# First blocks' last 64 features on VectorE, their fronts in another order, first weight jobs in other sizes, second block's end later

## The chip, the cores and the metric

One core of a Trainium2 chip runs the kernel. The metric is the device time of one execution in microseconds, the median of several runs. Engines: PE (TensorE; PEld is its weight load), DVE (VectorE), ACT (ScalarE), POOL (GpSimd) and SP (SyncE, which here only issues transfers).

## What is computed

Three layers, one after the other, on 2 x 4096 tokens of 192 features in float32:

```python
w = softmax(weight)                       # 8 heads x 7 taps; 24 features share a head
x = causal depthwise convolution of x with w, 7 taps
gate = 1 / (1 + exp(-(x @ w_gate)))       # 192 x 1536
x = (gate * (x @ w_val)) @ w_out          # 1536 x 192
h = x @ w_in                              # 192 x 2048
x = where(h > 0, h, exp(min(h, 0)) - 1) @ w_out2    # 2048 x 192
```

The weights arrive as 64-bit floats.

## The kernel before

**Tiling.** Tokens are cut into 16 blocks of 512. A block's 192 features lie as tiles of 128 rows: n holds features 0 to 127, s the same with its two halves of 64 rows swapped (made by two transfers inside the chip), r the last 64 features, in both halves. A matmul here uses 64 rows of PE, and two of them, on the two halves, run side by side; that is what n, s and r are for. Every value is split in a high part with few bits and the rest (h = cast on ACT, l = value - h on DVE), and a product is taken as three of four partial products. The same holds for the weights: w1 (gate and value), w2 (out), w3 and w4 of the second layer, each as h and l.

**A step.** A step is (kind, block, j): kind 1 is the gated layer, kind 2 the other. `front` (L345) runs 18 matmuls of 64 x 512 into two banks: gate and value of 128 hidden features, or 2 x 128 of kind 2. ACT and DVE make g from them (e by sigmoid, g = e x value; or relu, exp and g), split g into gh and gl, and two steps later (LAG) `back` (L397) multiplies them with w2 or w4 into the banks a0 to a3. Blocks 0 and 1 go together: their steps alternate, and one `back` of 20 matmuls serves both. 24 steps of kind 1 for blocks 0 and 1 (about 3.2 us each), 12 for block 2, 16 of kind 2 for blocks 0 and 1, 8 for block 2; then the next group. `end1` takes a block's sums out of the banks and makes n, s, r of kind 2.

**The convolution.** Later blocks are convolved on DVE, seven instructions over a tile (`conv`, L167), in time for their steps. For blocks 0 and 1, whose values are wanted first, PE does it: `diagonal` (L127) makes diagonal matrices of the tap weights on ACT; `conv_first` (L214) takes the first 128 features of both blocks with 56 matmul records, `conv_third` (L236) the last 64 with 28 such records. `split` (L203) then makes h and l. Two matmuls on zeros stand ahead (L591).

**The weights.** A job (`prep_in` for w1 and w3, `prep_out` for w2 and w4, with `narrow`, L268) turns 64-bit weights into h and l: transfers bring the words into a tile s (two buffers; m in some cases), ACT takes t = |high word|, DVE makes h, then the unit t, then the rest and its low part, ACT casts h. The first six jobs (ROOM, L29) have 384 columns and work within the tile s or m. The later ones have 768 columns and first need a copy m<-s, shifted by two bytes, by a transfer inside the chip; there is one m.

**What sets the order.** The program is recorded by hand: for each half step the pieces due are written out. PREPARED says how many pieces of the jobs are due by which step, CONV at which steps a block's convolution goes on, `times` (L680) when the pieces of an end are. Each engine runs its instructions in this order, and SP sends transfers in it.

Of the kernel before, what the change touches and what calls it, by code (L numbers as in the profile page):

```python
# [28 lines left out]
ROOM = "ssmssm"  # L29
# [8 lines left out]
    (-18, 0), (-15, 10), (-13, 10), (-9, 18), (-5, 18), (-1, 21), (2.5, 31), (6.5, 48.5),  # L38
    (10.5, 65), (14.5, 74.5), (18.5, 89.5), (24, 99), (34.5, 126), (38, 127), (49.5, 160),
# [18 lines left out]
def conv_glu_elu_kernel(  # L58
# [154 lines left out]

    def conv_first():  # L214
# [21 lines left out]
    def conv_third(fold):  # L236


        diagonal(1, fold)
        x = xin_t[0, 1]  # L240
        banks = two_banks()
        for k, w in enumerate(diagonals[1]):
            for acc, rows in zip(banks, HALVES):
# [24 lines left out]
    def narrow(src, out, room):  # L268


        copied = room is None
# [462 lines left out]
```

## Time and profile before

| | us |
|---|---|
| median of 3 runs | 1194.4 (1194.36 to 1194.5) |
| the profiled execution | 1194.23 |
| its span, first to last instruction | 1192.2 |
| PE busy | 1185.0 (99%) |
| DVE busy | 844.0 (71%) |
| ACT busy | 788.7 (66%) |

Matmuls overlap and their ends are modelled, so PE's busy time is read by counts of matmuls and by starts. A timeline row has start, duration, engine, line, operation, what it writes and reads, and in brackets the idle time before it with what ended it. DVE and ACT are busy in part, but not evenly: the first 90 us hold most of the weight jobs.

### The profile page before, as it was taken

Reading aid. Unit: us, or ns where it says so; the run is one execution under the profiler, and the core shown is the slowest. Engines: PE = TensorE matmul, PEld = TensorE weight load, DVE = VectorE, ACT = ScalarE, POOL = GpSimd, SP = SyncE. Lnnn points to the kernel's source line nnn. Section 1 sums busy time; section 2 is a strip of 40 time slices with the busy share of each in tenths; the row PEclk is TensorE's granted clock in tenths of the full one; section 3 lists DMA queues with packets and bytes.
Section 4 is the critical chain, followed back from the end, with each engine's and each line's share of the span. In section 5 each row is a group of like instructions: output and inputs, shape, how many; then the busy total and the mean of one; then the engine's idle time right before and its main releaser. Section 6 shows DMA issues by size and latency. Waiting matters only on the chain.

```text
span 1192.2 us, 25068 instructions
## 1 busy us (share of the span) xinstructions
PE 1185.0 (99%) x10332; PEld 1111.3 (93%) x10332; DVE 844.0 (71%) x1282; ACT 788.7 (66%) x1378; POOL 79.7 (7%) x70
## 2 busy tenths in 40 slices
PE   9999999999999999999999999999999999999998
PEld 4989989888888899999999999999999999999998
DVE  7998689785447877477766677666766667765675
ACT  6556788854448886448854498545884468844686
POOL 0000000001001000011001010010100100001110
PEclk9999999999999999999999999999999999999999
DMA  6656340321001020111112011020110201111100
GB/s 168 215 184 190 103 133 28 90 54 45 5 24 46 19 63 19 28 37 45 28 36 53 12 45 45 19 63 4 43 45 20 63 11 35 45 36 28 28 15 19
DMA packets 31794, 65.26 MB, mean 55 GB/s; under 512 B 4480, under 2 KB 15744, under 8 KB 31680
## 3 DMA queue, kind: packets, MB, share of 16 engines
q1 hardware_dynamic: 31680, 63.66, 19.2%
q8 instruction: 81, 1.33, 0.5%
q14 instruction: 33, 0.27, 0.1%
HBM read 19.74 MB, written 6.29 MB: 22 GB/s over the span
## 4 chain that ended last, share of the span: by engine, by line
PE 95%; DVE 3%; ACT 1%; DMA 1%; issue 1%; DVEq 0%; ACTq 0%
PE ps L343 52%; PE a L343 41%; DMA m<-s 1%; DVE gl L394 1%; PE ps L223 1%; PE ps L244 1%; DVE g L367 0%; DVE g L381 0%; ACT e L378 0%; PE ps L591 0%; ACT e L377 0%; ACT gh L388 0%; DVE w2s L312 0%; DVE t L292 0%; DVE h L298 0%
## 5 line engine op out<-in xcount | busy, mean ns | idle before, releaser
L388 ACT CAST gh<-g 128x512 fp32r<-128x512 f32 x448 | 273.3, 619 | 189.6 <-DVE g L367 147.2
L394 DVE TENSOR_TENSOR gl<-g,gh 128x512 fp32r<-128x512 f32 x448 | 333.1, 757 | 76.6 <-ACT gh L388 64.3
L343 PE MATMUL a<-gh,w4s 64*128 64x512 f32 x1536 | 302.7, 387 | 0.0
L343 PE MATMUL a<-gl,w4s 64*128 64x512 f32 x1024 | 256.7, 387 | 0.2 <-DVE gl L394 0.2
L381 DVE SCALAR_TENSOR_TENSOR g<-e,ps 128x512 f32<-128x512 f32 x256 | 174.1, 686 | 110.2 <-ACT e L378 108.8
L343 PEld LDWEIGHTS a<-gh,w4s 64*128 64x128 f32 x1536 | 225.0, 184 | 8.7 <-ACT two L442 0.3
L343 PE MATMUL a<-gh,w2s 64*128 64x512 f32 x1152 | 230.7, 387 | 0.0
L367 DVE TENSOR_TENSOR g<-e,ps 128x512 f32<-128x512 f32 x192 | 131.6, 685 | 136.1 <-ACT e L365 135.7
L365 ACT ACTIVATE e<-ps 128x512 f32<-128x512 f32 x192 | 114.9, 598 | 160.8 <-PE ps L343 160.0
L343 PE MATMUL a<-gl,w2s 64*128 64x512 f32 x768 | 188.1, 387 | 0.4 <-DVE gl L394 0.4
L343 PEld LDWEIGHTS a<-gl,w4s 64*128 64x128 f32 x1024 | 171.3, 184 | 6.4 <-DVE gl L394 1.2
L343 PEld LDWEIGHTS a<-gh,w2s 64*128 64x128 f32 x1152 | 161.9, 184 | 6.4
L378 ACT ACTIVATE e<-e 128x512 f32<-128x512 f32 x256 | 161.9, 632 | 8.1
L377 ACT ACTIVATE e<-ps 128x512 f32<-128x512 f32 x256 | 150.6, 588 | 15.4 <-PE ps L343 14.7
L343 PE MATMUL ps<-xn,w1h 64*128 64x512 f32 x768 | 152.1, 387 | 0.7 <-DVE g L367 0.7
L343 PE MATMUL ps<-xs,w1h 64*128 64x512 f32 x768 | 151.8, 387 | 0.1
L343 PE MATMUL ps<-xr,w1h 64*128 64x512 f32 x768 | 145.0, 386 | 0.0
L343 PEld LDWEIGHTS a<-gl,w2s 64*128 64x128 f32 x768 | 121.1, 184 | 5.9 <-DVE gl L394 1.7
L343 PEld LDWEIGHTS ps<-xn,w1h 64*128 64x128 f32 x768 | 105.3, 184 | 6.0 <-DVE g L367 1.1
L343 PEld LDWEIGHTS ps<-xs,w1h 64*128 64x128 f32 x768 | 105.1, 184 | 4.7 <-DVE g L367 0.5
L343 PEld LDWEIGHTS ps<-xr,w1h 64*128 64x128 f32 x768 | 102.2, 184 | 4.5 <-DVE xr L209 0.2
L343 PE MATMUL ps<-xn,w1l 64*128 64x512 f32 x384 | 105.2, 386 | 0.0
(107 smaller groups left out, 1728.4 us busy)
## 6 DMA issues: line engine op xcount, KB each, us to landing
xs<-xn SPq DMA_DIRECT2D x61, 256.0 KB, 3.6
m<-s SPq DMA_DIRECT2D x14, 767.8 KB, 4.1
s<-in_w_dram SPq DMA_DIRECT2D x57, 128.0 KB, 3.0
three<-two SPq DMA_DIRECT2D x47, 128.0 KB, 2.2
s<-in_w_dram SPq DMA_DIRECT2D x6, 768.0 KB, 4.6
x<-in_xp_dram SPq DMA_DIRECT2D x16, 259.0 KB, 3.8
out_dram<-one SPq DMA_DIRECT2D x16, 256.0 KB, 2.0
xr<-xr SPq DMA_DIRECT2D x14, 256.0 KB, 3.2
```

The lines of the kernel that those rows point to most:

```text
L223: nc.tensor.matmul(acc[to], w[rows, rows], x[rows, k:k + TB], start=k == 0, stop=k == TAPS - 1)
L244: nc.tensor.matmul(acc, w[rows], x[rows, k:k + TB], start=k == 0, stop=k == TAPS - 1)
L343: return nc.tensor.matmul(ps, w, x, start=first, stop=last)
L365: nc.scalar.activation(s, gate, AF.Sigmoid)
L367: nc.vector.tensor_mul(g, s, val)
L377: nc.scalar.activation(e, h, AF.Relu, scale=-1.0)
L378: nc.scalar.activation(e, e, AF.Exp, scale=-1.0)
L381: nc.vector.scalar_tensor_tensor(g, e, -1.0, h, ALU.add, ALU.max)
L388: nc.scalar.copy(gh, g)
L394: nc.vector.tensor_sub(gl, g, f32(gh))
```

## The change

1. `conv_third` runs on DVE, one multiply and six multiply-adds for the two blocks' 64 features at once, one cast, one subtraction; two transfers make the swapped copy. The 28 matmuls, the second set of diagonals and the matrix `fold` at the start go. Two more matmuls on zeros follow `conv_first`.
2. The x loads of blocks 0 and 1 are issued by ACT, the 64 features' loads by SP directly behind the tap weights.
3. The fronts of the first four steps begin with the parts that no transfer inside the chip makes (n and r for block 0, s and r for block 1), two of them one after the other, and their swapped parts follow. Block 1's first two fronts use the banks a0 to a3.
4. The first jobs: w1 0 and 1 (384 columns), w1 2 and 3 as one job of 768 in m without a copy, w2 0 and 1 (384), then all with a copy; w2 in jobs of 2, 4, 4 and 2.
5. PREPARED and CONV have other numbers. Block 1's end of kind 1 goes on four steps later.

```diff
-ROOM = "ssmssm"
+ROOM = [("s", False), ("s", False), ("m", True), ("s", False)]
...
-    (10.5, 65), (14.5, 74.5), (18.5, 89.5), (24, 99), (34.5, 126), (38, 127), (49.5, 160),
+    (34.5, 127), (38, 129), (49.5, 157),
...
-            nc.sync.dma_start(t, xp[0:P, bi, t0:t0 + TB + PAD])
+            (nc.scalar if b < 2 else nc.sync).dma_start(t, xp[0:P, bi, t0:t0 + TB + PAD])
...
+    def zeros(ps, n):
+        for _ in range(n):
+            nc.tensor.matmul(ps, warm[0][:, 0:P], warm[0], start=True, stop=True)
...
+        zeros(ps_a.tile([P, TB], F32, tag="a3", name="a3"), 2)
         yield
...
-    def conv_third(fold):
...
-        diagonal(1, fold)
+    def conv_third():
...
         x = xin_t[0, 1]
-        banks = two_banks()
-        for k, w in enumerate(diagonals[1]):
-            for acc, rows in zip(banks, HALVES):
-                nc.tensor.matmul(acc, w[rows], x[rows, k:k + TB], start=k == 0, stop=k == TAPS - 1)
-        yield
-        for b in range(2):
-            parts(1, b, "r")
-        yield from split([parts_t[1, b]["r"][0] for b in range(2)], banks)
-        yield
+        acc = xcv.tile([P, TB], F32, tag="xcv1", name="xcv")
+        for k in range(TAPS):
+            w, xk = cwn[:, 1, k:k + 1], x[:, k:k + TB]
+            if k:
+                nc.vector.scalar_tensor_tensor(acc, xk, w, acc, ALU.mult, ALU.add)
+            else:
+                nc.vector.tensor_scalar_mul(acc, xk, w)
+            yield
+        t, other = (xsp.tile([P, 2, TB], F32R, tag="r", name="xr") for _ in HALVES)
...
+        nc.scalar.copy(t[:, 0], acc)
+        yield
+        nc.vector.tensor_sub(t[:, 1], acc, f32(t[:, 0]))
+        for rows, to in zip(HALVES, HALVES[::-1]):
+            nc.sync.dma_start(f32(other)[to], f32(t)[rows])
+        yield
...
-        most, n = 6 * P, 3 * P * (1 + copied)
+        most, n = 6 * P, src.shape[0] * src.shape[2]
...
-        n = slice(n, n + 1 + (room is None))
+        n = slice(n, n + 1 + (room is None or room[1]))
...
-        jobs = [(index[1, 0, j], prep_in, w1d, w1, j) for j in (0, 1, 2, 3, 4, 6, 8, 10)]
-        jobs += [(index[1, 1, j] + LAG, prep_out, w2d, w2s, j) for j in (0, 2, 4, 8)]
+        jobs = [(index[1, 0, j], prep_in, w1d, w1, j) for j in (0, 1, 2, 4, 6, 8, 10)]
+        jobs_2 = [(index[1, 1, j] + LAG, prep_out, w2d, w2s, j) for j in (0, 2, 6, 10)]
...
-        next(jobs[0])
-        next(jobs[1])
         next(load_x(0, 1))
-        next(jobs[2])
+        for n in (0, 1, 2, 2):
+            next(jobs[n])
...
+                if i == 0:
+                    ps = front(w1, 0, parts_t[1, 0], ("nr", "s"), some=range(6))
+                    spare.append(front(w1, 0, parts_t[1, 1], ("sr", "n"), banks(0), range(6)))
+                    return front(w1, 0, parts_t[1, 0], ("nr", "s"), ps, range(6, 9))
+                if i == 1:
+                    return front(w1, 1, parts_t[1, 0], ("nr", "s"))
+                if i == 2:
+                    return front(w1, 0, parts_t[1, 1], ("sr", "n"), spare.pop(), range(6, 9))
+                return front(w1, 1, parts_t[1, 1], ("sr", "n"), banks(2))
...
-                    times = (0.5, 1, 2.5, 3, 3.5) if k == 1 else (0.5, 2.5)
+                    times = (0.5, 2.5) if k == 2 else (4.5, 5, 6.5, 7, 7.5) if b == 1 else (0.5, 1, 2.5, 3, 3.5)
```

**The order on DVE at the start,** from the tap weights (cwn) on; xcv is the convolution's tile, t, h, s and w1l are a weight job's. Before:

```order
L119 TENSOR_TENSOR cwn<-cwe,cwd 128x14
L292 TENSOR_SCALAR t<-t 128x384
L294 TENSOR_SCALAR t<-t 128x384
L298 SCALAR_TENSOR_TENSOR h<-s,t 128x384
L300 TENSOR_SCALAR t<-h 128x384
L306 TENSOR_SCALAR s<-s 128x384
L307 SCALAR_TENSOR_TENSOR s<-s 128x384
L312 SCALAR_TENSOR_TENSOR w1l<-s,t 128x384
L292 TENSOR_SCALAR t<-t 128x384
L294 TENSOR_SCALAR t<-t 128x384
L298 SCALAR_TENSOR_TENSOR h<-s,t 128x384
```

Now, on DVE from the same instruction on:

```order
L121 TENSOR_TENSOR cwn<-cwe,cwd 128x14
L257 TENSOR_SCALAR xcv<-x_104,cwn 128x512
L255 SCALAR_TENSOR_TENSOR xcv<-x_104,cwn,xcv 128x512 x6
L309 TENSOR_SCALAR t<-t 128x384
L311 TENSOR_SCALAR t<-t 128x384
L315 SCALAR_TENSOR_TENSOR h<-s,t 128x384
L264 TENSOR_TENSOR xr<-xcv,xr 128x512
L317 TENSOR_SCALAR t<-h 128x384
L323 TENSOR_SCALAR s<-s 128x384
L324 SCALAR_TENSOR_TENSOR s<-s 128x384
L329 SCALAR_TENSOR_TENSOR w1l<-s,t 128x384
L309 TENSOR_SCALAR t<-t 128x384
```

The seven convolution instructions and the xr split stand ahead of the first job's end and of the xn and xs splits; the two xr splits from banks, further down before, are gone.

**The order on PE around the first fronts** (gh, gl in the first rows are the diagonals; w1h, w1l the weights). Before, the last diagonal matmuls and the first front's start:

```order
L244 MATMUL ps<-x_112,gh 128x512 x8
L244 MATMUL ps<-x_112,gl 128x512 x6
L343 MATMUL ps<-xn,w1h 128x512
L343 MATMUL ps<-xs,w1h 128x512
L343 MATMUL ps<-xn,w1h 128x512
L343 MATMUL ps<-xs,w1h 128x512
L343 MATMUL ps<-xn,w1l 128x512
L343 MATMUL ps<-xs,w1l 128x512
L343 MATMUL ps<-xs,w1h 128x512 x4
L343 MATMUL ps<-xs,w1l 128x512 x2
L343 MATMUL ps<-xr,w1h 128x512 x4
L343 MATMUL ps<-xr,w1l 128x512 x2
```

Now, on PE from the added zeros (warm) behind the first 128 features' matmuls on:

```order
L218 MATMUL a_179<-warm 128x512 x2
L360 MATMUL ps<-xn,w1h 128x512
L360 MATMUL ps<-xs,w1h 128x512
L360 MATMUL ps<-xn,w1h 128x512
L360 MATMUL ps<-xs,w1h 128x512
L360 MATMUL ps<-xr,w1h 128x512 x4
L360 MATMUL ps<-xn,w1l 128x512
L360 MATMUL ps<-xs,w1l 128x512
L360 MATMUL ps<-xr,w1l 128x512 x2
L360 MATMUL a_258<-xs,w1h 128x512
L360 MATMUL a_259<-xn,w1h 128x512
L360 MATMUL a_258<-xs,w1h 128x512
```

The 14 rows' worth of diagonal matmuls on x_112 are gone, r stands ahead of the swapped part, and block 1's first front (a_258, a_259, which are a0 and a1) follows before block 0's is complete; the swapped part (xs in both banks) comes behind it, ten rows below the last one shown.

**The order on DVE at the end of block 2's kind 1 steps** (t, h, m of w3's third job; L381 and L400 make g of kind 2). Before:

```order
L367 TENSOR_TENSOR g<-e,ps 128x512
L292 TENSOR_SCALAR t<-t 128x768
L394 TENSOR_TENSOR gl<-g,gh 128x512
L367 TENSOR_TENSOR g<-e,ps 128x512
L394 TENSOR_TENSOR gl<-g,gh 128x512
L381 SCALAR_TENSOR_TENSOR g<-e,ps 128x512 x2
L394 TENSOR_TENSOR gl<-g,gh 128x512 x2
L381 SCALAR_TENSOR_TENSOR g<-e,ps 128x512 x2
L447 TENSOR_TENSOR one<-a_1511,one 128x512
L447 TENSOR_TENSOR two<-a_1512,two 128x512
L394 TENSOR_TENSOR gl<-g,gh 128x512 x2
L381 SCALAR_TENSOR_TENSOR g<-e,ps 128x512 x2
```

Now, on DVE at the same place, from the same g on:

```order
L386 TENSOR_TENSOR g<-e,ps 128x512
L309 TENSOR_SCALAR t<-t 128x768
L311 TENSOR_SCALAR t<-t 128x768
L315 SCALAR_TENSOR_TENSOR h<-s,t 128x768
L413 TENSOR_TENSOR gl<-g,gh 128x512
L386 TENSOR_TENSOR g<-e,ps 128x512
L317 TENSOR_SCALAR t<-h 128x768
L413 TENSOR_TENSOR gl<-g,gh 128x512
L386 TENSOR_TENSOR g<-e,ps 128x512
L321 TENSOR_SCALAR m<-m 128x768
L413 TENSOR_TENSOR gl<-g,gh 128x512
L400 SCALAR_TENSOR_TENSOR g<-e,ps 128x512 x2
```

The job's steps t, t, h, t, m stand ahead of kind 2's first g; before, its first t alone does.

## Rows read from the trace of the kernel before

**Rows 1.** The page's table of engines: busy us, share, instructions.

```profile
PE 1185.0 (99%) x10332; PEld 1111.3 (93%) x10332; DVE 844.0 (71%) x1282; ACT 788.7 (66%) x1378; POOL 79.7 (7%) x70
```

**Rows 2.** Windows, L343 alone: from:to, us, PE busy (count), granted clock, DMA share, GB/s.

```profile
18.14:32.81 14.67, 13.89 (x110) 1.00 0.64 174
32.81:89.74 56.93, 56.49 (x492) 1.00 0.61 200
89.74:136.24 46.50, 46.50 (x413) 1.00 0.60 182
136.24:216.49 80.25, 79.40 (x671) 1.00 0.22 73
216.49:1187.40 970.91, 970.91 (x8564) 1.00 0.14 35
...
136.24:150.37 14.13, 13.49 (x114) 1.00 0.09 20
```

**Rows 3.** Windows, DVE alone; columns as in rows 2.

```profile
89.20:136.00 46.80, 36.79 (x62) 1.00 0.60 180
146.70:165.00 18.30, 17.52 (x30) 1.00 0.46 134
23.10:89.20 66.10, 64.74 (x114) 1.00 0.60 192
```

**Rows 4.** Timeline of DVE: start, us, what.

```profile
3.62 0.17 DVE L119 TENSOR_TENSOR cwn<-cwe,cwd 128x14 f32<-128x14 f32 x1
7.14 0.36 DVE L292 TENSOR_SCALAR t<-t 128x384 f32<-128x384 f32 x1 [3.35 <-ACT t L285]
7.54 0.36 DVE L294 TENSOR_SCALAR t<-t 128x384 int32<-128x384 int32 x1
7.93 0.56 DVE L298 SCALAR_TENSOR_TENSOR h<-s,t 128x384 int32<-128x384 int32 x1
...
23.08 0.68 DVE L367 TENSOR_TENSOR g<-e,ps 128x512 f32<-128x512 f32 x1
```

**Rows 5.** Timeline of ACT, SP and PE.

```profile
0.74 1.28 ACT L115 ACT_TABLE_LOAD   x1 [0.74 <-PEq L719]
1.19 0.90 SPq L160 DMA_DIRECT2D x<-in_xp_dram  x2
...
18.14 0.79 PE L343 MATMUL ps<-xn,w1h 64*128 64x512 f32 x1
...
32.81 0.75 PE L343 MATMUL ps<-xn,w1h 64*128 64x512 f32 x4
```

**Rows 6.** The chain that ended last: start, us, what.

```profile
12.49 6.21 PE ps L244 x28
```

**Rows 7.** Lines L175 and L179 (convolution of later blocks): count, ns min/median/max.

```profile
L175 DVE SCALAR_TENSOR_TENSOR xcv<-x,cwn,xcv x126: 739/745/787, 46.1 to 1062.4; 128x512 f32<-128x512 f32 x126
...
L179 DVE TENSOR_SCALAR xcv<-x,cwn x19: 478/480/484, 176.2 to 1041.8; 128x512 f32<-128x512 f32 x19
```

**Rows 8.** DMA issues, 0 to 25 us: count, KB each, median us to landing.

```profile
x<-in_xp_dram SPq DMA_DIRECT2D x2, 129.5 KB, 3.0
...
xs<-xs SPq DMA_DIRECT2D x1, 256.0 KB, 4.1
```

**Rows 9.** DVE's groups by shape, 0 to 90 us: busy us, mean ns, idle before.

```profile
L298 DVE SCALAR_TENSOR_TENSOR h<-s,t 128x768 int32<-128x768 int32 x7 | 6.7, 953 | 0.1
L294 DVE TENSOR_SCALAR t<-t 128x768 int32<-128x768 int32 x7 | 3.9, 553 | 0.1
```

**Rows 10.** Waits of PEld, 100 to 216 us: total us, times, longest.

```profile
PEld ps L343 <- DVE g L381: 2.7, 6, 0.8
PEld a L343 <- DVE gl L394: 1.2, 3, 0.7
```

**Rows 11.** Waits over the whole span.

```profile
DVE m L304 <- DMA m<-s: 0.6, 2, 0.3
```

**Rows 12.** Tile m, 0 to 80 us, its transfers.

```profile
DMA to landing us min/median/max: 2.7/4.0/5.2
```

More of the change, by code (lines that the diff above doesn't have):

```diff
@@ L343, in mm, with front @@
         return nc.tensor.matmul(ps, w, x, start=first, stop=last)
-    def front(w, n, x, first):
+    def front(w, n, x, order, ps=None, some=range(9)):
         h, l = (t[:, n] for t in w)
-        ps = [ps_w.tile([P, TB], F32, tag="w", name="ps") for _ in HALVES]
+        ps = ps or [ps_w.tile([P, TB], F32, tag="w", name="ps") for _ in HALVES]
         todo = []
-        for two in ("nsr" if first else ("nr", "s") if w is w1 else ("ns", "r")):
+        for two in order:
             todo += [(part, 0, k) for part in two for k in (0, 1)] + [(part, 1, 0) for part in two]
         for at, (part, low_w, low_x) in enumerate(todo):
+            if at not in some:
+                continue
             wt = l if low_w else h
@@ L551, in conv_glu_elu_kernel @@
         needs, sizes = [x[0] for x in jobs], [6 + (x[1] is prep_out) for x in jobs]
-        takes = [1.0 if n < len(ROOM) else 1.35 for n, size in enumerate(sizes) for _ in range(size)]
+        takes = [1.45 if n == 2 else 1.0 if n < len(ROOM) or x[1:] == jobs_2[3][1:] else 1.35
+                 for n, (x, size) in enumerate(zip(jobs, sizes)) for _ in range(size)]
         jobs = [x[1](*x[2:], dict(enumerate(ROOM)).get(n)) for n, x in enumerate(jobs)]
@@ L562, in weights @@
                 for k, _ in enumerate(f):
-                    if k == (2 if n < 3 else sizes[n] - 1) and n + 1 < len(jobs):
+                    if k == (2 if n == 0 else sizes[n] - 1) and n + 1 < len(jobs):
                         next(jobs[n + 1])
@@ L570, in weights @@
                     next(jobs[n + 1])
-                if one and n + 3 < len(ROOM) + 2:
-                    next(jobs[n + 3])
-                    if n + 3 >= len(ROOM):
-                        next(jobs[n + 3])
+                if one and n != 2:
+                    m = n + 3 - (n == 3)
+                    next(jobs[m])
+                    if m >= len(ROOM):
+                        next(jobs[m])
                 if not one and n + 2 < len(jobs):
@@ L599, in conv_glu_elu_kernel @@
         prepared = weights()
-        for k in range(-40, 2 * len(steps)):
+        for k in range(2 * int(PREPARED[0][0]), 2 * len(steps)):
             for (a, m), (b, n) in zip(PREPARED, PREPARED[1:]):
@@ L618, in conv_glu_elu_kernel @@
         for (b, i), pieces in CONV.items():
-            f = conv(b, i) if b else conv_third(fold) if i else conv_first()
+            f = conv(b, i) if b else conv_third() if i else conv_first()
             if b > 1:
@@ L627, in conv_glu_elu_kernel, with banks @@
         held = {}
+        spare = []
+        def banks(n):
+            return [ps_a.tile([P, TB], F32, tag=f"a{i}", name=f"a{i}") for i in (n, n + 1)]
         for i in range(int(min(extra)) - 1, len(steps) + LAG + 2):
```

44 lines of the change are left out of this document (25 added, 19 removed).

## The prediction

> **What bounds the kernel now.** I read the page's table of engines first: PE is busy for 99% of the span [rows 1], so only time in which PE has no wide matmul to run can be won. Then the windows with the wide matmuls alone (all of `front` and `back`, one line) [rows 2]. From 216 us to the end 8564 of them take 970.91 us, 0.1134 us each, with nothing lost. At that price the other stretches lose: 18.14 to 32.81 us 14.67 - 110 x 0.1134 = 2.2 us; 32.81 to 89.74 us 56.93 - 492 x 0.1134 = 1.1; 89.74 to 136.24 us minus 0.3 (about three matmuls counted reach in from the stretch before); 136.24 to 216.49 us 80.25 - 671 x 0.1134 = 4.2. With those three taken off their counts the second and the fourth lose 1.5 and 4.5 us. Ahead of all this lie 18.14 us without a wide matmul [rows 5]. The change touches these stretches and leaves the rest alone.
>
> What ends the waits is VectorE. From the first g at 23.08 us to 89.2 us it is busy 64.74 of 66.10 us, from 146.7 to 165 us 17.52 of 18.30 [rows 3], and between 100 and 216 us PE waits 2.7 us for its g and 1.2 us for its gl [rows 10]. Earlier it stands still for 3.35 us, until the first weights have come at 7.14 us [rows 4]. So up to 90 us the kernel is a VectorE queue that starts at 7.14 us. PE's own start is the chain of diagonal matmuls, the last 28 of which (the 64 features) take 6.21 us [rows 6].
>
> **The 64 features' matmuls go.** PE loses 6.21 us of work ahead of its first wide matmul. That is no gain by itself: the first front needs xn and xs split, and these now stand behind more work on VectorE.
>
> **The convolution on VectorE.** One multiply of 480 ns and six multiply-adds of 745 ns [rows 7]; each reads what the last one wrote, and such a successor starts some 0.04 us after the end (7.14 + 0.36, then 7.54 [rows 4]): 0.48 + 6 x 0.785 = 5.2 us. When can it begin? The tap weights are ready at 3.62 + 0.17 = 3.8 us [rows 4]. ScalarE now issues two loads ahead of its table load, which took 1.28 us from 0.74 us on; no row shows an issue on ScalarE, but SP takes 0.90 us for these two [rows 5], so exponential and weights come some 0.2 us later: 4.0 us. The 64 features are now SP's second and third transfer, the latter issued at about 1.7 us; such transfers took 3.0 us [rows 8]: 4.7 us. Bounds: 4.0 (landed earlier) and 5.8 (4.1 us, the slowest transfer of rows 8, though that one stays on the chip). I take 4.7, the same kind of transfer. The convolution then ends at 9.9 us. Of its 5.2 us, 2.4 lie in the time in which VectorE stood idle; the other 2.8 push the weights back. One of the two xr splits (0.69 us) goes, and so does about 1 us of waits for ScalarE.
>
> As to those loads, a rule of the Trainium skill speaks against a gain ("DMA: Bandwidth & Descriptors", Issuing engines are not separate DMA queues): whichever engine issues, the same 16 DMA engines carry it, and only issue time is saved. By that rule the x loads would crowd the 64 features', towards the late bound; no row here has two issuers at once. With 5.8 for 4.7 us the sum below would be 1.1 us higher.
>
> **From there to the sixth front.** Ahead of its first g VectorE has two jobs of 384 (each 4 x 0.36 + 3 x 0.56 us [rows 4] = 3.1), six steps of a job of 768 (4 x 0.55 + 2 x 0.95 [rows 9] = 4.1) and three splits of 0.69: 12.4 us. Independent neighbours overlap by some 0.08, dependent ones lose 0.04, which leaves 11.9: the first g at 21.8 us instead of 23.08. PE is no later limit for it: the swapped parts leave when xs is split (9.9 + 6.1 = 16.0 us) and land 4.1 us later [rows 8], at 20.1; with three pairs of matmuls and the sigmoid, g's input is there at 21.7 us. From this g to the fourth VectorE has 17 instructions (seven g, gl of 0.69, one 768 of 0.95, a 384 job, a 0.55), 9.0 us start to start, and one wait: the second e stands behind a cast and a t on ScalarE, 0.9 us. So the fourth g ends at 21.8 + 9.9 = 31.7. It empties the bank a3, which the first `back` needs, because the second block's first fronts now use the a banks; then 7 of that back's 10 pairs remain, 7 x 0.227 = 1.6 us. **The sixth front starts at 33.3 us instead of 32.81 [rows 5]: +0.5.** PE begins earlier and is stopped harder: it waits for the splits, for the swap and for that g, some 1.5 us each time.
>
> **From the sixth front to 89.7 us.** The jobs in other sizes save VectorE time. Between the first g and that of step 20 the new order has, against the old, one 768 multiply-add more (+0.9 us), two 384 less (-1.0), one 384 and two 768 single steps less (-1.3) and two small ones of w2s less (-0.6): 2.0 us less. Before, this stretch filled VectorE; now it falls below PE's pace, and gl is ready 1 to 1.6 us ahead of need. Against it stand the copies m<-s: each may start only when the job before is through with m, it lands in 4.0 us (2.7 to 5.2 [rows 12]), and VectorE asks for it in order. Two jobs (w1 from 4, w1 from 8) have only 3.7 to 4.2 us between; 0.8 to 1 us of standing each, which the lead covers but for some 0.3. Before, all copies together cost 0.6 us [rows 11]. **1.5 lost becomes 0.3: -1.2.** Bounds: -1.5, and 0 (the waits eat the lead).
>
> **From 136 to 216 us.** Five of the six steps of w3's third job now stand ahead of the first fronts of the second kind; before, one did. With what follows from it 2.4 us less of VectorE lie in this stretch. They go to block 2's twelve steps, which get ten 768 instructions more, 6 us; VectorE was busy 36.79 of 46.80 us there [rows 3], so nothing waits. The 4.5 us are not all theirs: up to 150.37 us 14.13 - (114 - 3) x 0.1134 = 1.5 us are lost [rows 2], at the switch of kinds, where e, exp, g and the sums follow one another; these stay. Of the other 3.0 I take **-1.0**, since ScalarE is in those chains too; bounds 0 and -1.9. The second block's end comes four steps later (`times`); that moves three VectorE instructions within the roomy stretch, and its result is used five steps after it is done: nothing.
>
> **Sum.** +0.5 - 1.2 - 1.0 = -1.7 us on the profiled 1194.23 us: 1192.5. The median of the runs, 1194.4, lies 0.2 above: 1192.7, and I say **1192.6 us**, between the two.
>
> **Rivals.**
> 1. *The freed VectorE time is worth all of itself.* Convolution at 4.0 us (-0.7 against the sum), no wait for copies (-0.3), the late stretch at its bound (-0.9): 1190.7. For it: VectorE is full in every stretch that loses. Against: its waits run through ScalarE too.
> 2. *Moved, not removed.* The copies eat the lead (+1.2) and the late stretch is ScalarE's (+1.0): 1194.8, no change. For it: a VectorE step counts only where nothing else is late.
> 3. *Slower: the copy queue.* Place: 30 to 43 us. SP now sends four blocks of w2 and their copy, six fetches for w1 of 0.6 us each, three more, two x loads and the next copy in one row, all behind the swaps. I have that copy land at 42.5 us, 0.8 after VectorE asks. Each us later stops VectorE, and beyond 1.5 us of lead PE; the next copies follow in its wake. Slower than before from about 3 us later on; with 5 us, 3.5 us are lost here and 1 at the job from 8: 1197.1. Against it: all copies before cost 0.6 us [rows 11].
> 4. *The clock.* Waits of 1.5 us between 14 and 31 us could cost PE its rate. In the rows the granted clock is 1.00 (the 2.4 GHz level) in every stretch [rows 2]. At the lower level (1.2 GHz) 40 wide matmuls cost 40 x 0.1134 = 4.5 us more: 1197.1. The Trainium skill ("TensorE: Matmul & The Clock Gate", Why this matters for your kernels) warns that gaps between bursts put PE back to the slow level; by that rule this could happen, and the trace, with shorter gaps, does not show it.
>
> **How the numbers follow.** About 0.2%, 2.4 us, is what a measurement of this kernel can tell from no change: faster means below 1192.0, slower above 1196.8. My forecast (1191.3 to 1193.9) has 0.49, a quarter of it below 1192.0; rival 1 has 0.24, rival 2 0.14, rival 3 0.08, rival 4 0.05. Faster 0.24 + 0.12 = 0.36; slower 0.08 + 0.05 = 0.13; same 0.51. The range for 8 in 10 goes from 1190.2, rival 1 and a little, to 1195.9, the sum with the late bounds (+1.1, +1.2, +1.0); it leaves out rivals 3 and 4 and the tail below.
>
> **What would show it.** Right: VectorE's first multiply at 4.5 to 5 us; the first g near 21.8, the sixth front near 33.3 us; 0 to 0.5 us lost from there to 90 us, 3 to 4 between 136 and 216 us; the first wide matmul well ahead of 18.14 us without gain from it. Wrong: a granted clock below 1; VectorE standing more than 2 us for m; or a sixth front before 32 us, which would mean that the walk has an order or a landing too late.

## The result: 0.9% slower

The changed kernel takes 1204.95 us, median of 6 runs (1203.88 to 1205.4); the kernel before, beside it, 1194.45. The ratio is 1.0088, interval 1.0075 to 1.01: 10.5 us more where 1.8 less were forecast, and outside the range. One of the kernel before's six runs took 2001.79 us; it counts as slow, and the ratio is that of the others. The profiled execution took 1204.93 us. The page's table of engines, to be held against [rows 1]:

```profile
PE 1187.6 (99%) x10308; PEld 1151.1 (96%) x10308; DVE 848.9 (71%) x1280; ACT 785.7 (65%) x1368; POOL 77.6 (6%) x66
```

Busy time tells little: but for PEld no engine has over 5 us more work, and PEld's sum is no measure (1151.1 us here, 1077.2 in e2_late below, with the same weight loads). The windows of the wide matmuls alone (L360 now), cut at the changed kernel's first wide matmul, at its sixth front, at 89.74 and 136.24 us as in [rows 2], and where its last 8564 begin (from:to, us, PE busy (count), PEld busy (count), granted clock, DMA share, GB/s):

```profile
13.80:36.59 22.79, 18.62 (x111) 14.24 (x113) 0.78 0.62 181
36.59:89.74 53.15, 50.48 (x430) 45.94 (x428) 1.00 0.51 168
89.74:136.24 46.50, 45.93 (x400) 41.97 (x398) 1.00 0.65 195
136.24:227.21 90.97, 88.31 (x747) 79.99 (x744) 1.00 0.26 84
227.21:1198.00 970.79, 970.79 (x8564) 964.46 (x8563) 1.00 0.14 35
```

The first wide matmul starts at 13.80 in place of 18.14 us, as forecast without gain: 111 of them then take 22.79 us, at a granted clock of 0.78. The last 8564 take 970.79 us as before. In between, too few matmuls fit into each window.

Since all kernels run the same 10240 wide matmuls, the clearest measure is when the Nth of them starts, in order of starts. The table gives that time minus the kernel before's, in us, from one profile of each kernel. Number 110 (counted from 0) opens the sixth front, 440 starts at 71.7 us before, 542 at 83.3, 962 at 131.0, 1140 at 153.0, 1680 at 216.8. The last columns are the times (median; ratio to the kernel before, 95% interval).

| kernel | 110 | 440 | 542 | 962 | 1140 | 1680 | us | ratio |
|---|---|---|---|---|---|---|---|---|
| changed | +3.8 | +3.3 | +7.1 | +10.2 | +11.5 | +10.7 | 1204.95 | 1.0075 to 1.0100 |
| e1_zeros | +5.0 | +4.0 | +6.8 | +10.7 | +11.6 | +10.7 | 1204.31 | 1.0069 to 1.0100 |
| e2_late | +2.0 | +2.5 | +6.1 | +6.1 | +5.8 | +6.0 | 1201.86 | 1.0049 to 1.0079 |
| e3_times | +2.3 | +2.2 | +5.6 | +10.2 | +10.5 | +9.8 | 1204.18 | 1.0071 to 1.0104 |
| e4_earlier | +3.6 | +3.2 | +3.6 | +6.8 | +8.0 | +7.3 | 1202.56 | 1.0055 to 1.0085 |
| e5_base | +3.9 | +3.6 | +4.0 | +4.0 | +3.6 | +3.8 | 1197.93 | 1.0018 to 1.0040 |
| e6_loads | +2.5 | +3.2 | +3.7 | +3.7 | +3.3 | +3.4 | 1196.98 | 1.0014 to 1.0032 |
| e7_pe_conv | +3.1 | +2.6 | +3.1 | +3.4 | +3.1 | +3.2 | 1197.45 | 1.0022 to 1.0042 |
| e11_pe_conv_t | +3.2 | +2.8 | +3.1 | +3.4 | +3.1 | +3.3 | 1197.52 | 1.0018 to 1.0038 |
| e8_fronts | +3.7 | +4.7 | +5.2 | +5.2 | +4.8 | +5.0 | 1199.20 | 1.0028 to 1.0056 |
| e13_bank | +3.5 | +3.4 | +3.9 | +3.9 | +3.6 | +3.7 | 1197.16 | 1.0015 to 1.0037 |
| e16_zeros2 | +2.3 | +3.0 | +3.5 | +3.5 | +3.1 | +3.3 | 1197.26 | 1.0017 to 1.0038 |
| e14_jobs | +1.7 | +2.5 | +2.9 | +4.2 | +3.9 | +4.0 | 1198.33 | 1.0023 to 1.0049 |
| e15_mended | +0.1 | +0.8 | +1.2 | +1.3 | +1.0 | +1.1 | 1196.33 | 1.0009 to 1.0028 |
| e17_w2_earlier | +1.5 | +2.4 | +2.8 | +2.9 | +2.5 | +2.8 | 1195.27 | 1.0004 to 1.0022 |
| e9_start | +5.3 | +5.3 | +5.3 | +5.2 | +5.2 | +5.2 | 1199.88 | 1.0032 to 1.0062 |
| e10_start_loads | +4.1 | +3.7 | +3.7 | +3.6 | +3.6 | +3.6 | 1198.20 | 1.0021 to 1.0047 |
| e18_start_mended | +3.0 | +2.8 | +2.8 | +2.7 | +2.7 | +2.7 | 1197.64 | 1.0020 to 1.0043 |
| e12_before_late | -0.4 | -0.2 | -0.2 | -0.3 | +0.9 | -0.3 | 1194.68 | 0.9993 to 1.0013 |

The changed kernel loses in three places: 3.8 us ahead of the sixth front, 3.8 between matmuls 440 and 542 (75 to 90 us), 3.1 between 542 and 962 (90 to 141 us); of 1.3 more at the switch of kinds 0.8 come back behind it.

The start, on DVE (timeline; to be held against [rows 4]):

```profile
4.43 0.17 DVE L121 TENSOR_TENSOR cwn<-cwe,cwd 128x14 f32<-128x14 f32 x1
6.25 0.49 DVE L257 TENSOR_SCALAR xcv<-x,cwn 128x512 f32<-128x512 f32 x1 [1.65 <-DMA x<-in_xp_dram]
6.77 4.69 DVE L255 SCALAR_TENSOR_TENSOR xcv<-x,cwn,xcv 128x512 f32<-128x512 f32 x6
11.38 0.35 DVE L309 TENSOR_SCALAR t<-t 128x384 f32<-128x384 f32 x1
...
24.02 0.69 DVE L386 TENSOR_TENSOR g<-e,ps 128x512 f32<-128x512 f32 x1 [0.62 <-ACT e L384]
...
33.12 0.68 DVE L386 TENSOR_TENSOR g<-e,a 128x512 f32<-128x512 f32 x1
```

On PE (timeline), where it stops:

```profile
17.01 0.79 PE L360 MATMUL ps<-xn,w1h 64*128 64x512 f32 x1 [2.23 <-DVE xn L211]
...
31.81 0.73 PE L360 MATMUL a<-gh,w2s 64*128 64x512 f32 x3 [1.40 <-ACT e L384]
...
33.26 0.79 PE L360 MATMUL a<-gl,w2s 64*128 64x512 f32 x1 [0.54 <-DVE gl L413]
...
36.59 0.67 PE L360 MATMUL ps<-xn,w1h 64*128 64x512 f32 x3
```

And what the clock did (windows of all engines: PE, PEld, DVE, ACT, POOL busy (count), granted clock, DMA share, GB/s):

```profile
15.00:17.00 2.00, 0.00 (x0) 0.00 (x0) 1.88 (x6) 1.35 (x4) 0.00 (x0) 0.80 0.94 228
17.00:23.00 6.00, 5.99 (x27) 4.55 (x29) 5.79 (x11) 0.72 (x1) 0.00 (x0) 0.50 0.97 254
23.00:30.00 7.00, 7.00 (x65) 6.38 (x62) 5.38 (x11) 4.96 (x10) 0.00 (x0) 1.00 0.57 207
30.00:33.40 3.40, 1.46 (x10) 0.62 (x6) 3.33 (x9) 1.58 (x3) 0.00 (x0) 0.98 0.01 2
33.40:37.00 3.60, 3.60 (x18) 2.69 (x20) 3.56 (x7) 1.56 (x3) 0.00 (x0) 0.55 0.64 188
```

PE started early, stopped for the splits (2.23 us) and was granted the 1.2 GHz level (0.50) from 17 to 23 us; it stopped again at the first back, and fell a second time.

One profile is one execution, and the clock differs from one to the next. Up to the sixth front e2_late (below) runs the same program and stops for the same times (2.23, 1.59 and 0.54 us). Its profile shows a shorter first fall and no second (columns as above):

```profile
17.00:23.00 6.00, 5.77 (x33) 4.42 (x35) 5.79 (x12) 1.22 (x3) 0.00 (x0) 0.72 0.94 254
33.00:37.00 4.00, 3.91 (x34) 3.60 (x34) 3.93 (x8) 2.18 (x4) 0.00 (x0) 1.00 0.67 196
```

Its number 110 is 2.0 us late and not 3.8, e3_times' 2.3. So the longer first fall and the second cost 1.5 to 1.8 us there, and 110 can differ by as much between two executions of one start. In the time they cost less: the changed kernel's two runs with a mean clock of 0.999 took 1203.88 and 1204.17 us, its four with 0.996 or 0.997 1204.93 to 1205.40.

The second place, in the chain that ended last (start, us, what):

```profile
67.38 0.34 DVE w2s L329
67.72 0.48 DVE t L309
68.20 0.06 SPq L306
68.25 0.06 issue
68.31 0.60 SPq L283
68.92 0.04 issue
68.96 1.34 SPq L283
70.29 0.04 issue
70.33 4.57 DMA s<-in_w_dram
74.90 0.02 issue
74.93 0.90 ACT t L302
```

When w2's job from 6 lets m go (67.7 us), SP sends the copy of w1's job from 8 (L306) and behind it the fetch for the job from 10, which lands at 74.9. ACT makes its t only then, and the gl that PE needs stands behind that t on DVE. DVE's timeline there, and its waits for m over the whole span (total us, times, longest; [rows 11] had 0.6):

```profile
72.41 0.56 DVE L321 TENSOR_SCALAR m<-m 128x768 int32<-128x768 int32 x1 [0.96 <-DMA m<-s]
73.00 0.96 DVE L329 SCALAR_TENSOR_TENSOR w1l<-m,t 128x768 fp32r<-128x768 int32 x1
75.85 0.56 DVE L309 TENSOR_SCALAR t<-t 128x768 f32<-128x768 f32 x1 [1.89 <-ACT t L302]
```

```profile
DVE m L321 <- DMA m<-s: 3.8, 4, 1.3
```

In the third place the same happens with w3's and w4's jobs (waits, 89 to 150 us):

```profile
PEld a L360 <- DVE gl L413: 3.5, 6, 1.4
DVE m L321 <- DMA m<-s: 2.1, 2, 1.3
ACT t L302 <- DMA s<-in_w_dram: 1.9, 1, 1.9
```

### The profile page after: what moved, and what is told of

It is laid out like the page before. It is cut to its first block, busy times and chain, and to the rows that moved or that the text cites. A ratio compares the mean times of both kernels' runs of the same rounds, so it can differ in the third digit from the quotient of the medians.

```text
span 1203.1 us, 24993 instructions
## 1 busy us (share of the span) xinstructions
PE 1187.6 (99%) x10308; PEld 1151.1 (96%) x10308; DVE 848.9 (71%) x1280; ACT 785.7 (65%) x1368; POOL 77.6 (6%) x66
## 4 chain that ended last, share of the span: by engine, by line
PE 92%; DVE 3%; ACT 2%; DMA 1%; issue 1%; SPq 0%; DVEq 0%; ACTq 0%
PE ps L360 51%; PE a L360 41%; DMA s<-in_w_dram 1%; DVE g L386 1%; DVE gl L413 1%; ACT e L397 0%; DVE xcv L255 0%; DVE h L315 0%; ACT e L384 0%; SPq L283 0%; DMA x<-in_xp_dram 0%; ACT e L396 0%; ACT gh L407 0%; DVE g L400 0%; DVE t L309 0%
## 5 line engine op out<-in xcount | busy, mean ns | idle before, releaser
L360 PE MATMUL a<-gh,w4s 64*128 64x512 f32 x1536 | 299.1, 387 | 0.0
L400 DVE SCALAR_TENSOR_TENSOR g<-e,ps 128x512 f32<-128x512 f32 x256 | 174.4, 686 | 108.0 <-ACT e L397 106.1
L360 PE MATMUL a<-gl,w4s 64*128 64x512 f32 x1024 | 249.6, 387 | 0.2 <-DVE gl L413 0.2
L360 PE MATMUL a<-gh,w2s 64*128 64x512 f32 x1152 | 230.1, 389 | 1.4 <-ACT e L384 1.4
L360 PEld LDWEIGHTS a<-gh,w4s 64*128 64x128 f32 x1536 | 217.6, 184 | 2.2 <-ACT two L461 0.3
L360 PE MATMUL a<-gl,w2s 64*128 64x512 f32 x768 | 187.3, 390 | 2.1 <-DVE gl L413 2.1
L360 PEld LDWEIGHTS a<-gh,w2s 64*128 64x128 f32 x1152 | 161.4, 185 | 4.6 <-ACT e L384 1.8
L360 PEld LDWEIGHTS a<-gl,w4s 64*128 64x128 f32 x1024 | 161.8, 184 | 1.9 <-DVE gl L413 1.0
L360 PE MATMUL ps<-xn,w1h 64*128 64x512 f32 x756 | 148.0, 389 | 5.2 <-DVE xn L211 2.2
L360 PE MATMUL ps<-xs,w1h 64*128 64x512 f32 x764 | 148.1, 388 | 0.0
L360 PE MATMUL ps<-xr,w1h 64*128 64x512 f32 x760 | 142.1, 388 | 0.0
L360 PEld LDWEIGHTS a<-gl,w2s 64*128 64x128 f32 x768 | 119.1, 185 | 6.1 <-DVE gl L413 4.5
L360 PEld LDWEIGHTS ps<-xn,w1h 64*128 64x128 f32 x756 | 103.3, 185 | 10.2 <-DVE g L386 3.7
L360 PEld LDWEIGHTS ps<-xs,w1h 64*128 64x128 f32 x764 | 104.7, 185 | 2.0 <-DVE xs L211 0.3
L360 PEld LDWEIGHTS ps<-xr,w1h 64*128 64x128 f32 x760 | 101.7, 185 | 1.6
L360 PE MATMUL ps<-xs,w1l 64*128 64x512 f32 x382 | 101.4, 387 | 0.0
```

The source lines that it names most:

```text
L360: return nc.tensor.matmul(ps, w, x, start=first, stop=last)
L400: nc.vector.scalar_tensor_tensor(g, e, -1.0, h, ALU.add, ALU.max)
```

## Experiments: where the pieces lie

These four are edits of the changed kernel.

**e1_zeros.** Three more zeros behind the first convolution, three ahead of the first back (`banks`' a0).

```diff
-        zeros(ps_a.tile([P, TB], F32, tag="a3", name="a3"), 2)
+        zeros(ps_a.tile([P, TB], F32, tag="a3", name="a3"), 5)
...
+                if kind_k == 1 and j_k == 0 and not spare:
+                    spare.append(zeros(ps_a.tile([P, TB], F32, tag="a0", name="a0"), 3))
```

> The changed kernel with five matmuls on zeros behind the first convolution in place of two, and three more on zeros ahead of the first back, so that PE does not stand between 14.8 and 17 us and between 30.5 and 33 us. Theory A (the fall of the granted clock to the 1.2 GHz level, 16.4 to 23 us and 33.4 to 36.7 us, is on the path): the clock stays at the 2.4 GHz level, the sixth front starts near 34 us in place of 37.09, the time falls to about 1202. Theory B (VectorE's queue sets the pace there and the clock is only a by-product): the clock may stay up, the sixth front stays within 1 us of 37.1 and the time within 1 us of 1204.9. Theory C (the zeros come in the way themselves): later than 37.1 us.

C: number 110 comes 1.2 us later still, at no gain in time. The clock stayed at 1.00 from 17 to 23 us, but the first front started at 16.53 us, and the clock fell from 23 to 30 us (0.76) instead. (The 37.09 us of the expectation is the front's third pair; its first is at 36.59.)

**e2_late, e3_times, e4_earlier.** Three edits of when pieces are due.

```diff
-    (34.5, 127), (38, 129), (49.5, 157),
+    (34.5, 122.5), (38, 123.5), (49.5, 157),
```

> The changed kernel, but the numbers of PREPARED from step 24 on lowered (122.5 at 34.5, 123.5 at 38), so that five of the six pieces of w3's third job come behind the switch of kinds again, as in the kernel before, and the others between steps 24 and 34 by half a step to a step later. Theory A (block 2's twelve steps of kind 1 hold too much work for VectorE with the one copy tile): 2 to 3 of the 3.5 us lost between 90 and 150 us come back, and up to 1 us is lost behind 150 us: about 1203. Theory B (it is the second block's end, which now lies in those steps, not the weight jobs): 1205, within 0.7 us.

```diff
-                    times = (0.5, 2.5) if k == 2 else (4.5, 5, 6.5, 7, 7.5) if b == 1 else (0.5, 1, 2.5, 3, 3.5)
+                    times = (0.5, 2.5) if k == 2 else (0.5, 1, 2.5, 3, 3.5)
```

> The changed kernel, but with the second block's end at its old place (0.5 to 3.5 steps behind the sums, with block 0's). Theory A (the weight jobs alone fill block 2's steps): no change, 1205 within 0.7 us, and what is won at 118 to 139 us is lost at 103 to 111 us, where both ends come together. Theory B (the end's three VectorE and three ScalarE instructions and its four transfers make gl late at 121.9, 128.9 and 139.7 us): 1.5 to 2.5 us less, about 1203.

```diff
-(6.5, 45.5), (10.5, 54), (13.5, 63), (14.5, 71.5)
+(6.5, 45.5), (9.5, 54), (12, 63), (14.5, 71.5)
```

> The changed kernel, but with the pieces of w1 from 6, w2 from 6 and w1 from 8 half a step to one and a half steps earlier (54 at step 9.5, 63 at step 12), so that w1 from 8 is not done in one step behind w2 from 6. Theory A (the one copy tile and the fetch behind it are what stops PE by 2.4 us at 77 us and 0.9 us at 86 us, since two jobs follow each other at once): PE's stop at 77 us is under 0.7 us and the time 1202 to 1203. Theory B (VectorE simply has too much work up to 90 us, wherever the pieces lie): the stop moves to another place, the time within 0.7 us of 1204.9.

e2: theory A. From 542 to 962 nothing is lost (3.1 in the changed kernel), and DVE's waits for m between 89 and 150 us fall from 2.1 to 0.3 us. e3: theory A, the end's place is not it; the loss only moves. e4: theory A. From 440 to 542 0.4 us are lost in place of 3.8, and PEld's waits for g between 60 and 90 us are, in the changed kernel and in e4:

```profile
PEld ps L360 <- DVE g L386: 2.4, 2, 1.3
```

```profile
PEld ps L360 <- DVE g L386: 0.5, 1, 0.5
```

**e5_base.** Both edits of e2 and e4.

> The changed kernel with both corrections of the weight jobs' times at once: those of e2_late (from step 24 on) and of e4_earlier (steps 9.5 to 14.5). Theory A (the two losses, 3.2 us between 90 and 150 us and 3.3 us around 77 us, are separate and both come from where PREPARED puts the pieces): they add up, the time falls by 6 to 7 us to about 1198, and what is left against the kernel before, some 4 us, was lost ahead of the sixth front. Theory B (they are one queue, and what is won ahead is waited away behind): 1201 to 1203, as each alone.

A: they add up, 7.0 us less than the changed kernel. So two thirds of the loss were numbers in PREPARED. The start's 3.9 us are left (3.65 by the medians).

## Experiments: the start

All but e9, e10, e18 and e12 are edits of e5_base.

**e6_loads.** All x loads on SP, the 64 features' first.

```diff
-            (nc.scalar if b < 2 else nc.sync).dma_start(t, xp[0:P, bi, t0:t0 + TB + PAD])
+            nc.sync.dma_start(t, xp[0:P, bi, t0:t0 + TB + PAD])
...
+        next(load_x(0, 1))
         next(load_x(0, 0))
         next(load_x(1, 0))
-        next(load_x(0, 1))
```

> e5_base, with all x loads on SP and the 64 features' two loads ahead of the others, so that ScalarE issues nothing ahead of its table load. Theory A (the loads crowd one another, whoever issues them, and the 64 features' came 1.4 us late for that): the first multiply of the convolution starts near 5.0 us in place of 6.25, the weights' work and the sixth front move up by about 1.2 us, and the time is 1 to 1.5 us under that of e5_base. Theory B (these transfers take that long in any order, or the first convolution on PE, whose loads now come last, takes its place): the time within 0.7 us of e5_base.

The 64 features' loads in the changed kernel, and in e6 (issues, 0 to 10 us: count, KB each, median us to landing):

```profile
x<-in_xp_dram SPq DMA_DIRECT2D x2, 129.5 KB, 4.4
```

```profile
x<-in_xp_dram SPq DMA_DIRECT2D x2, 129.5 KB, 2.8
```

The convolution starts at 4.68 us, its end comes 1.6 and the sixth front 1.4 us earlier, but 0.4 are left at number 440, and the medians differ by 0.95 us with overlapping intervals. Theory A for the loads; most of the gain is lost again behind the sixth front.

**e7_pe_conv, e11_pe_conv_t.** The convolution back on PE (`conv_third(fold)`, `fold` and the second diagonals as before, no added zeros), with

```diff
-    (0, 1): [-38 + k for k in range(7)] + [-26.5, -25],
+    (0, 1): [-29, -8.5, -8],
```

and, in e11, -26.5 for -29.

> e5_base, but with the 64 features' convolution back on PE (28 matmul records, the second set of diagonals and fold as before, no zeros behind the first convolution); loads, fronts and jobs as changed. Theory A (VectorE is the queue that sets the start, and its convolution pushes the first weight job from 7.1 to 11.4 us): VectorE's first weight instruction is back near 7.5 us, the sixth front 2 to 4 us earlier than in e5_base, the time 1194 to 1196. Theory B (the fronts' new order or the job sizes delay the sixth front, not the convolution): the time within 0.7 us of e5_base; worse than that if PE's 6.2 us come back.

> e7_pe_conv (e5_base with the 64 features' convolution on PE), but with the second set of diagonals on ScalarE behind the first weight job's t and not ahead of it, as in the kernel before; in e7_pe_conv VectorE's first weight instruction came at 9.6 us for that. Theory A (the start is VectorE's queue, from its first weight instruction on): that instruction is back near 7.3 us, the sixth front 1.5 to 2.5 us earlier than the 35.9 us of e7_pe_conv, the time near 1195.5. Theory B (the job sizes and the fronts' order set it): the sixth front within 0.7 us of e7_pe_conv, the time within 0.7 us of 1197.4.

Both theories A fall. In e11 DVE's first weight instruction comes at 8.45 us, 2.9 earlier than in the changed kernel, yet number 110 only 0.7 us earlier than in e5, less than two executions of one start can differ by. PE's timeline of e11 shows the same stop at the first back:

```profile
31.21 0.73 PE L351 MATMUL a<-gh,w2s 64*128 64x512 f32 x3 [1.72 <-ACT e L375]
```

**e8_fronts.** The old order and banks of the fronts.

```diff
-                if i > 3:
-                    return front(w1, j, parts_t[1, b], ("nr", "s"))
...
+                return front(w1, j, parts_t[1, b], ("nr", "s") if i else ("nsr", ))
```

> e5_base, but with the first four fronts in the old order and in the old banks (n, s, r; block 1's first two not in the banks a0 to a3). Theory A (VectorE's queue sets the start, the fronts' order does little): the first wide matmuls are later, the sixth front within 0.7 us of e5_base, the time within 0.7 us of it. Theory B (the new order makes the first back wait for the fourth g, since that front's bank is a3, and starts PE so early that it stops and drops to its 1.2 GHz level): no fall of the granted clock behind 23 us, the sixth front 1.5 to 3 us earlier, the time lower by as much. Theory C (the new order was worth something): 1 to 3 us above e5_base.

A for the sixth front (0.2 us earlier than e5's), C in the time (1.3 us above e5). What e8 loses against e5 it loses between 110 and 440 (from +3.7 to +4.7, where e5 goes from +3.9 to +3.6). There DVE stands 2.3 us for the copy for w1 from 4 (0.9 in e5). Why that copy comes later with the old order was not tested.

**e9_start, e10_start_loads.** The kernel before with items 1, 2 and 3 of the change, and that with e6's loads.

> The kernel before with the start of the changed one alone: the 64 features' convolution on VectorE, the x loads on ScalarE, the zeros and the first four fronts' order and banks; the weight jobs with their old sizes and times, and the old end. Theory A (VectorE's convolution ahead of the first weight job is what delays the start): its first weight instruction near 11.4 us, the sixth front at 35 to 36.5 us, 1196.5 to 1198. Theory B (the sizes of the first jobs delay it: a 768 job ahead of the first of w2, whose low part the first back waits for until 32.1 us): the sixth front at 33.5 us or earlier, 1193.5 to 1194.7.

> e9_start, with all x loads on SP and the 64 features' two ahead of the others. Theory A: as in e6_loads the convolution starts 1.5 us earlier, and the sixth front and the time come 1 to 1.5 us under e9_start. Theory B (the first back waits for something else): the time within 0.5 us of e9_start.

e9: worse than either theory; with the old jobs the new start loses 5.2 us. e10: theory A, the loads give 1.6 of them back (1.7 by the medians).

**e13_bank, e14_jobs, e15_mended, e16_zeros2.** The fourth front in the rotating banks; the whole old start with the new jobs; e6 and e13 together; three zeros ahead of the first back alone (second half of e1's edit).

```diff
-                return front(w1, 1, parts_t[1, 1], ("sr", "n"), banks(2))
+                return front(w1, 1, parts_t[1, 1], ("sr", "n"))
```

> e5_base, but the fourth front writes two of the four rotating banks, as in the kernel before, and not a2 and a3; only block 1's first front stays in a0 and a1. Theory A (the first back stands because the fourth step's sigmoid and g have to empty a2 and a3 first; e7_pe_conv and e11_pe_conv_t, with VectorE's weights 2 to 3 us earlier, started the sixth front no earlier for that): the wait for that sigmoid and g ahead of the first back goes, the sixth front starts 1.5 to 2.5 us earlier than 36.6, the second fall of the clock goes with it, and the time is 1196 to 1196.7. Theory B (the first back waits for gl and for w2's low part on VectorE just as long): the sixth front and the time within 0.7 us of e5_base.

> e5_base with the whole start of the kernel before (PE convolution of the 64 features, the old order and banks of the fronts, the x loads on SP in the old order): what is left of the change are the weight jobs' other sizes, their times as in e5_base, CONV of block 2 and the later end. Theory A (all that is lost ahead of the sixth front comes from convolution, loads, fronts and banks): the sixth front at 32.5 to 33.5 us, the time 1193.5 to 1194.7. Theory B (the 768 job ahead of the first of w2 delays g and gl by some 1.5 us as well): the sixth front at 34 to 35 us, 1195 to 1196.5.

> e5_base with both remedies that leave the convolution on VectorE: all x loads on SP with the 64 features' first (as e6_loads), and the fourth front in the rotating banks (as e13_bank). Theory A (late loads and banks are two costs that add up): the sixth front near 33.5 us, 1194.5 to 1195.5. Theory B (VectorE's queue, 2.7 us later than before even so, sets gl and w2's low part): the time within 0.7 us of e6_loads, 1196.3 to 1197.7.

> e5_base with three matmuls on zeros, into bank a0, ahead of the first back alone, where PE stands from 30.4 to 33.8 us. Theory A (the fall of the granted clock to the 1.2 GHz level behind that stop costs the 1.6 us by which the rest of the first back and the next front are slower): no fall between 33 and 38 us, the sixth front 1.2 to 1.8 us earlier, the time about 1196.5. Theory B (the slow matmuls lie in time that would be waited anyway): no fall, the time within 0.5 us of e5_base's 1197.9.

e13, B in the main: the bank is free, but number 110 is only 0.4 us earlier, since gl (to 33.2 us) comes nearly as late as the fourth g did (33.8); the clock falls again, and the median is 0.77 us under e5's, with overlapping intervals. e14: even the old start is 1.7 us late with the new job sizes, as B says, and 0.8 us more are lost up to 440, 1.3 more from 542 to 962, which takes the time beyond B's range. e16: no fall of the clock from 33.4 to 37 us,

```profile
33.40:37.00 3.60, 3.60 (x35) 3.57 (x33) 3.56 (x7) 1.89 (x4) 0.00 (x0) 1.00 0.72 198
```

35 matmuls for 18; number 110 is 1.5 us earlier, 0.5 of that is left at 1680, and the time cannot be told from e5's. It is not shown that the zeros do this: e2's and e3's profiles have no zeros there and the same clock, and four of e16's nine runs have the mean clock (0.996 or 0.997) of runs with two falls. What the falls cost is better read from runs of one kernel: e5's three at 0.998 or 0.999 took 1196.46 to 1197.32 us, its four at 0.995 or 0.996 1197.93 to 1198.39, 1.3 us more by the medians. e15, between A and B: with loads and bank mended the clock stays at 1.00, and number 110 is level with the kernel before, in a profile that is the fastest of its ten runs (1195.34 us). Then 1.1 us are lost; by a wait on DVE this is the copy for w1 from 4 (timeline of e15):

```profile
43.29 0.56 DVE L321 TENSOR_SCALAR m<-m 128x768 int32<-128x768 int32 x1 [1.91 <-DMA m<-s]
```

**e17_w2_earlier.** e15 with that copy asked for earlier.

```diff
-(2.5, 28), (5.5, 38), (6.5, 45.5)
+(2.5, 29), (4.5, 38), (6.5, 45.5)
```

> e15_mended, but with the pieces of w2 from 2 and of w1 from 4 half a step to one step earlier (29 at step 2.5, 38 at step 4.5), so that the copy for w1 from 4 is issued earlier than at 37.5 us; in e15_mended it landed at 43.3, VectorE stood 1.9 us for it, and PE lost 1.9 us between 37 and 51 us. Theory A (the copy of that job is the loss, as at 77 us): VectorE's wait for m falls under 0.7 us, 1 to 1.5 us come back, the time about 1195.2. Theory B (the pieces delay the first g's and gl's by as much as the copy gains): the time within 0.5 us of 1196.3.

Median 1.06 us under e15: theory A by the median, with intervals that overlap. The profiled execution was its slowest (1197.06). It shows 0.6 us for m but the loss elsewhere, and it differs from e15's ahead of anything that the edit touches: from 7 to 9 us PE gets through 9 diagonal matmuls where e15's did 20, and the first wide matmul starts at 16.64 us, not 15.02. So the trace does not settle it. This is the best form found of the change, and 0.13% (0.04 to 0.22) slower than the kernel before.

**e18_start_mended.** e10 with e13's bank.

> e10_start_loads (the kernel before with the 64 features' convolution on VectorE, all x loads on SP with theirs first, the new fronts) with the fourth front in the rotating banks. Jobs, PREPARED and the ends are those of the kernel before. Theory A (with loads and banks mended the new start is as good as the old one, and what e15_mended still loses is the job sizes' copy): no fall of the clock, the sixth front at 32.5 to 33.5 us, the time 1193.5 to 1195. Theory B (with the old jobs VectorE's convolution still costs 2 us): the sixth front at 34 to 35 us, 1196 to 1197.

B, and more (the sixth front at 35.8 us, the time above 1197): the new start does not suit the old jobs, mended or not.

**e12_before_late.** The prediction's third term alone, on the kernel before.

```diff
-    (34.5, 126), (38, 127), (49.5, 160),
+    (34.5, 131.5), (38, 133), (49.5, 160),
```

> The kernel before with one thing of the change: the numbers of PREPARED from step 24 on raised (131.5 at 34.5, 133 at 38), so that five of the six pieces of w3's third job come ahead of the switch of kinds and the pieces from step 26 on half a step to two steps earlier. Theory A (the prediction's term: VectorE's work moved into block 2's roomy steps is won behind the switch): 0.5 to 1.5 us less than before, near 1193.3, with no more lost between 90 and 136 us. Theory B (the copies through the one m do not keep up when the jobs follow one another closer, and the switch's own chain takes what is won behind it): 1 to 4 us more than before, with VectorE standing for m between 100 and 140 us.

Neither: no change. The copies keep up here. Behind number 1140 1.2 us are won, and 1.2 are lost at the switch. ACT's timeline of e12 suggests why:

```profile
139.65 0.83 ACT L318 CAST w3h<-h 128x768 fp32r<-128x768 f32 x1
140.38 0.91 ACT L285 ACTIVATE t<-s 128x768 f32<-128x768 f32 x1
141.20 0.58 ACT L377 ACTIVATE e<-ps 128x512 f32<-128x512 f32 x1
```

and of the kernel before:

```profile
139.94 0.59 ACT L377 ACTIVATE e<-ps 128x512 f32<-128x512 f32 x1
```

The job's last piece is also a cast on ACT, and the next job's t follows it; both now stand ahead of the e of kind 2's second front, 1.26 us later, in the one chain that PE waits for there. This is read from the two traces; no run moves those two pieces back.

## Why the prediction was wrong

**To the sixth front (+0.5; measured +3.8).** The walk's order and durations held: six multiply-adds took 4.69 us (4.71 by the estimate), and from the convolution's start on each time is where it was put, once three inputs are mended. (1) The loads: start at 6.25 us, not 4.7, and past the late bound of 5.8. The prediction took a landing of 3.0 us from a trace in which SP alone issued; with ACT beside it, it is 4.4. The rule of the Trainium skill that it weighed ("DMA: Bandwidth & Descriptors", Issuing engines are not separate DMA queues) agrees with this trace, and e6 shows it: +1.55. (2) The first fall of the clock makes the first sigmoid late, DVE waits 0.62 for it: 21.8 + 1.55 + 0.62 = 24.0, measured 24.02. (3) The fourth g then ends at 33.8 (31.7 + 2.2), and the rest of the back takes 36.59 - 33.86 = 2.7 us at the lower level and not 1.6. 33.3 + 1.55 + 0.62 + 1.1 = 36.6. In e2 the first g starts at 23.42 us with no wait for the sigmoid, and the clock does not fall behind it. Without the two clock terms, and with its loads (convolution from 6.36 us, 1.66 late), the sum gives 33.3 + 1.66 = 35.0, and its sixth front starts at 34.8. So two steps failed: a landing of 3.0 us that measured 4.4, and a clock that was held constant. The text saw the stops, priced the fall as a rival with 0.05 and named a clock below 1 as a sign of being wrong; it came twice, in its place. The Trainium skill ("TensorE: Matmul & The Clock Gate", Why this matters for your kernels) warns that gaps put PE back to the slow level, but it speaks of longer gaps than these. Here stops of 2.23 us and less went ahead of the falls, and the measurement decides.

**33 to 90 us (-1.2; up to matmul 542 +3.3).** Here the failed step is "which the lead covers but for some 0.3". It walked the two copies, and not the fetch that SP sends behind a copy for the job after, nor ACT's t that waits for it, nor the gl behind that t. 2 us less work on DVE gained nothing, since the pieces of two jobs fell due within one step. e4 shows it: the same work, spread, loses 0.4. The gain of 1.2 is in no run even so: from number 110 to 542 e4 and e5, whose pieces are spread, come out at 0.0 and +0.1, and where number 110 is early (e6, e15, e17) 1.1 to 1.3 are lost again. DVE then stands for the copy for w1 from 4 (1.9 us in e15, 0.7 in the changed kernel); that this is the cause is read from the wait, not tested.

**136 to 216 us (-1.0), and 90 to 136 us (nothing).** "VectorE was busy 36.79 of 46.80 us there, so nothing waits" was the worst step: a share of busy time says nothing of a chain through one tile m. DVE is not full there in the changed kernel either (to be held against [rows 3]):

```profile
89.20:136.00 46.80, 39.20 (x66) 1.00 0.64 192
```

Yet 3.1 us were lost between 542 and 962. e2 keeps six of the ten added job instructions in block 2's steps and loses nothing, so more work alone does not cost it; with e4 beside it, what costs is how closely the jobs follow one another. VectorE stood 3.8 us for m over the span, the second of the prediction's own signs of being wrong. And the gain behind the switch is given back at it (e12; by ACT, as the timelines read): the term is 0 even where copies keep up.

**Rivals.** The third, the copy queue, was the right mechanism in the wrong place (68 to 78 and 118 to 139 us, not 30 to 43) and came in two places; its 0.08 and its price were too small. The copy that it named, for w1 from 4, landed at 45.8 us (42.5 by the prediction) and cost a wait of 0.7 us. With the fourth it makes up most of the loss: 7.0 of the 10.5 us go with the times of the jobs (e5), the clock's falls are about 1 (the changed kernel's own runs), and the late loads may be 1 more (e6, by the medians). What the remaining 1 to 2 us are is open.

**What stays open.** Why the old start with the new jobs (e14) and the new start with the old jobs (e9, e18) both lose 3.6 to 5.7 us and the two new ones together, mended, only 1.3 to 2.3 (medians): DVE's order may fit the one pair better, but no run takes single instructions apart. The runs of e15 and e17 scatter over some 2 us, as those of the kernel before do beside them (1.5 to 1.9). What makes the first diagonal matmuls of e17's profile later than e15's is open, and so is what sets how long a fall of the clock lasts in one execution and not in the next.

## What to carry to other kernels

An engine's idle share is no room for work that passes through a serial resource: walk fetch, copy, the other engine's piece and the consumer behind it, for the job after the moved one too. Work that is moved takes its parts on other engines along. And a start that lets PE begin early but makes it stop twice can pay with its clock. One profile is one execution: the same start lost 2.0 us in one and 3.8 in another.

## What the hardware showed unexpectedly

The granted clock fell to the 1.2 GHz level after a stop of 2.23 us (14.8 to 17.0) and again after stops of 1.40 and 0.54 us around a few matmuls, where the kernel before, whose longest stop on PE from 18 to 34 us was 0.71 us, kept 1.00. The same stops did not always bring it: after 1.59 and 0.54 us e2's clock stayed at 1.00. Four loads from two issuing engines took 4.4 us for the smaller ones, against 2.8 us when SP issued all four and those two first.
